# Where the matmul operands of a two-part kernel lie in SBUF, modulo 256 bytes, and two buffers in place of three for one result

## The chip, the cores and the metric

The kernel runs on one core of one Trainium2 chip. The metric is the device time of one execution in microseconds (us). Before the change it is 1865.64 us, the median of three runs (1865.52 to 1867.26). A time below that is faster.

## The reference

For four sequences of 3072 positions with 256 features, three blocks follow one another:

```python
# 1: a real Fourier transform over the sequence, a complex 256x256 mix, soft threshold, inverse
X = np.fft.rfft(x, axis=1)
Yr = Xr @ w_r - Xi @ w_i + b_r
Yi = Xr @ w_i + Xi @ w_r + b_i
Y = sign(Y) * max(abs(Y) - 0.01, 0)          # on Yr and Yi apart
y = np.fft.irfft(Y, n=3072, axis=1)
# 2: 256 -> 2048 -> 256 with h * tanh(softplus(h)) between ("H" below)
h = y @ w_in;  z = (h * np.tanh(np.log1p(np.exp(h)))) @ w_out
# 3: channel mix, 256 -> 1024 -> 256 ("K" below)
xk = mu_k * z + (1 - mu_k) * z_prev;  xr = mu_r * z + (1 - mu_r) * z_prev
v = np.maximum(xk @ w_k, 0) ** 2 @ w_v
out = v / (1 + np.exp(-(xr @ w_r)))
```

`w_in`, `w_out`, `w_k`, `w_v` and the gate's `w_r` arrive as 8-byte floats; the kernel decodes them itself.

## The kernel before, in words

Two functions follow one another. `part1` does block 1, `part2` blocks 2 and 3. All matmuls are issued through `mm` (L211), ScalarE's copies and functions through `act` (L208), VectorE's operations through `tt` (L202) and `stt` (L205); rows are therefore told apart by tile names.

**Part 1** runs 48 steps `u` (4 sequences x 12 tiles of frequencies). In each step TensorE does the forward transform of tile `u + 1` (`emit_F`, PSUM tile `xps`), the mix of tile `u` (`emit_M`, `yps`) and the inverse transform of tile `u - 1` (`emit_I`, `bps`). ScalarE and VectorE work between them, in an order that the code writes out: `post_M` and `post_M2` are the soft threshold (`yb`, first on ScalarE, then on VectorE), `post_F` splits the transformed tile into a high part `xh` (ScalarE) and a low part `xl` (VectorE). `post_I(u - 2)` copies the inverse's result from PSUM to an SBUF tile `bs` (ScalarE) and sends it to DRAM (`b_dr`). `preload` puts the bias into the PSUM tile of a later mix (ScalarE). Between them VectorE works through a background queue: butterflies of the transform's short factor (tiles `a` and `g`) and decoding of weights. Each engine does its instructions strictly in the order in which they were issued. All DMAs are issued by one queue, SP's, in order too. The pool of the tile `bs` has three buffers, and the tile `warm` at the start takes one of them, so that the ScalarE copy of step `u` waits until the DMA of step `u - 3` has landed.

**Part 2** is issued by a planner (`Plan`) that orders steps by due times and estimated costs. Each big product is done as seven products of half-size blocks. Every operand is split into a high and a low fp32r part, and each product is three matmuls: high by high, high by low, low by high. There are two stages:

- H: 96 groups, each with 7 products (21 matmuls into `x`, `z`, `c`, `d`; stationary `wr`, 128 columns, moving `yc`, 512 columns) and 4 units of the second layer (6 matmuls each into `a`; stationary `wo`, moving `h` and `l`, 512 columns).
- K: 48 groups, each with 7 products (21 matmuls; stationary `wk`, moving `yc`, 512 columns), 4 units (12 matmuls each into `v`; stationary `h` and `l`, moving `wv`, 256 columns) and one gate unit (12 matmuls into `zps`; stationary `xr`, moving the gate's weights, 256 columns, which lie in the last `wk` tile of each quadruple).

Every stationary operand has 128 columns, 512 bytes of a partition.

"Place" below means the address within a partition, modulo 256 bytes, counted from the place at which all pools begin: the sizes of the pools are whole multiples of 256 bytes, but for the first small one, so all begin at the same place. Tiles of `mat` (weights) have 512 floats, 2048 bytes: place 0. In stage H everything lies at place 0. In stage K the helper `OFF` moves `yc` by 16 floats, and `outs_of` (its second argument) and the tile `xr` do the same with `h`, `l` and `xr`: place 64. So in stage K before:

- products: stationary `wk` at 0, moving `yc` at 64
- units and gate: stationary `h`, `l`, `xr` at 64, moving `wv` and gate weights at 0

The tiles `fm`, `im` of part 1 (transform matrices) and the weights of part 2 come from the same pool `mat` with 24 buffers, which are used in turn.

Of the kernel before, what the change touches and what calls it, by code (L numbers as in the profile page):

```python
# [11 lines left out]
F32 = mybir.dt.float32  # L12
# [157 lines left out]
def tile_fft_mix_moe_channel_mix(  # L170
# [53 lines left out]
    big = pool(ctx, "big", 2)  # L224
    mat = pool(ctx, "mat", 24)
    g_p = pool(ctx, "g", 1)
# [320 lines left out]
    def wout_piece(i):  # L547
        raw = raw_piece(w_out[256 * i:256 * i + 256, :])

        def parts(q):  # L550
            ts = [mat.tile([128, 2, 256], F32R, tag="m", name="wo") for _ in range(2)]
            wt["out", 2 * i], wt["out", 2 * i + 1] = ts
            return [(ts[k][:, 0, :], ts[k][:, 1, :], q[:, k, :]) for k in range(2)]
        return decode(raw, flat_q, parts)
# [78 lines left out]
    def new_ring(k):  # L633
        for _ in range(4):
            ring.append(mat.tile([128, 4, 128], F32R, tag="m", name="wr"))

# [5 lines left out]
    def part1():  # L642
        with ExitStack() as es:
# [3 lines left out]
            yb_p = pool(es, "yb", 2)  # L647
            bs_p = pool(es, "bs", 3)
            st_p = pools["st"] = pool(es, "st", 2)
# [113 lines left out]
            for i in range(NT + 1):  # L763
                if i < NT:
                    fm[ORD[i]] = mat.tile([128, 2, 256], F32, tag="m", name="fm")
                if 1 <= i:
                    im[ORD[i - 1]] = mat.tile([128, 2, 256], F32, tag="m", name="im")
            new_a(0)
# [64 lines left out]
            for u in range(NU):  # L833
# [62 lines left out]
                if u == NU - 2:  # L896
                    for c in (4, 5, 12, 13, 6, 7, 14, 15):
                        wt["out", c] = mat.tile([128, 2, 256], F32R, tag="m", name="wo")
                    new_ring(0)
                    for k in range(4):  # L900
                        load_ring(0, k)
# [9 lines left out]
    def part2():  # L911
        with ExitStack() as es:
# [8 lines left out]
            NA = 8 * NSB  # L921
            OFF = lambda key: 16 if key >= NSB else 0
            KINDS = [(0, 0), (0, 1), (1, 1), (1, 0)]
# [65 lines left out]

            def outs_of(second, off, f32_of, unit_of, cost):  # L990


                def outs(n, made):
                    b, T = at(n), at(n + 1) - at(n)
                    read = {}
                    for q, kind in enumerate(KINDS):
# [4 lines left out]
                        def tiles(kind=kind, st=st):  # L1001
                            if not st:
                                for i, w in enumerate("hl"):
                                    st[i] = o_p.tile([128, 576], F32R, tag="%s%d%d" % ((w,) + kind), name=w)[:, off:off + 512]
                            return st
# [53 lines left out]

            out_H = outs_of(units, 0, f32_H, unit_H, 1.362)  # L1060

            def moving(key, b0, pace, load, old, *prev):
# [14 lines left out]
                for q, k in enumerate(MOVING):  # L1077
                    def hi(k=k, q=q):
                        if q == 0:
                            mv[key] = big.tile([128, 7232], F32R, tag="big", name="yc")[:, OFF(key):OFF(key) + 7168].rearrange("p (a b f) -> p a b f", a=2, b=7)  # L1080
                        part_hi(mv[key], tl["s"], k)()
                    h = add("ACT", 0.54, b0 + 14 + pace * (q + 1), hi, sums[k] if k < 4 else ld, first or old)
                    first = first or h
                    l = add("DVE", 0.6, b0 + 14 + pace * (q + 1.5), lambda k=k: part_lo(mv[key], tl["s"], k)(), h)
                    res[q] = [h, l]
                    reads += [h, l]
# [172 lines left out]

            kw, vw, have = {}, {}, {}  # L1260
            held = [[units[8 * (NSB - 1) + c % 8, (i, c // 8)] for i in range(2)]
# [5 lines left out]
            for e, ((w, g, k), free) in enumerate(zip(want, held)):  # L1267
                def fetch(w=w, g=g, k=k):
                    if w == "v":
                        vw[g] = mat.tile([128, 2, 256], F32R, tag="m", name="wv")  # L1270
                        nc.sync.dma_start(out=vw[g].bitcast(F32), in_=v_dr[g // 2][:, :, 256 * (g % 2):256 * (g % 2) + 256])
                        return
                    t = mat.tile([128, 4, 128], F32R, tag="m", name="wk")
                    kw.setdefault(g, []).append(t)
                    m = 4 if k < 3 else 2
                    nc.sync.dma_start(out=t[:, 0:m, :].bitcast(F32), in_=k_dr[g][:, 4 * k:4 * k + m, :])
                    if k == 3:
                        s, h = divmod(g, 2)
                        nc.sync.dma_start(out=t[:, 2:4, :].rearrange("p a f -> p (a f)").bitcast(F32),
                                          in_=v_dr[4][:, s, 256 * h:256 * h + 256])  # L1280
# [36 lines left out]

            out_K = outs_of(vunits, 16, f32_K, unit_K, 1.412)

# [5 lines left out]
            def gate_prep(J, b0):  # L1325
                res, first = {}, None
                for i in range(2):
                    s = slice(512 * i, 512 * i + 512)

                    def load(s=s):  # L1330
                        if not xr:
                            xr[0] = g_p.tile([128, 4160], F32R, tag="g", name="xr")[:, 16:4112].rearrange(
                                "p (s h f) -> p s h f", s=2, h=2)
                        nc.sync.dma_start(out=xr[0][:, 1, :, s].bitcast(F32), in_=xr_dr[J].rearrange("h p f -> p h f")[:, :, s])
# [11 lines left out]
            def gate(J, q, need):  # L1346
# [6 lines left out]
                def go():  # L1353
                    ps = tl["p"] = psw.tile([128, 2, 256], F32, tag="z", name="zps")
                    for p in range(2):
                        ts = slice(256 * q + 128 * p, 256 * q + 128 * p + 128)
                        for h in range(2):
                            wh, wl = [kw[2 * s + h][3][:, 2:4, :].rearrange("p a f -> p (a f)") for s in range(2)]
                            xh, xl = [xr[0][:, s, h, ts] for s in range(2)]
# [80 lines left out]
```

## Time and profile before

| | |
|---|---|
| median of the runs | 1865.64 us |
| the profiled execution | 1865.58 us |
| its span, first to last instruction | 1863.8 us |
| TensorE (PE) busy | 1854.4 us, 99% |
| VectorE (DVE) busy | 1413.8 us, 76% |
| ScalarE (ACT) busy | 1197.3 us, 64% |
| mean granted TensorE clock | 1.000 |

Busy time of TensorE counts matmuls from their start to their modelled end, and neighbours overlap; a share of 99% says that a matmul is nearly always under way, not that each goes at the best rate. The rate is read from the starts: the time between the starts of consecutive matmuls. PEld is the loading of stationary operands, which runs beside the matmul before. Idle time of an engine stands with what ended it ("<-").

### The profile page before, as it was taken

To read this page: it belongs to the slowest core of one execution; us is meant where nothing else is said; L and a number is where in the kernel's file an instruction comes from. 1 tells how busy PE (TensorE), PEld (TensorE's weight loads), DVE (VectorE), ACT (ScalarE), POOL (GpSimd) and SP (SyncE) were. 2 spreads that over 40 slices of the span, in tenths; PEclk is the share of its full clock that TensorE was granted. 3 is DMA by queue.
4 is the path that set the end of the run, shared out by engine and by line. 5 is a ranking of instruction groups with operands and counts; after the bars stand their busy time and mean duration, and the time that the engine had idled before them with its cause. 6 is when DMAs were issued, how large, how long until landed. Compare 5 with 4: busy or idle time off the path is not lost.

```text
span 1863.8 us, 26630 instructions
## 1 busy us (share of the span) xinstructions
PE 1854.4 (99%) x9658; PEld 1597.8 (86%) x9658; DVE 1413.8 (76%) x2519; ACT 1197.3 (64%) x2151; POOL 5.9 (0%) x16
## 2 busy tenths in 40 slices
PE   9999999999999999999999999999999999999999
PEld 7888888888888888888888888888999999999998
DVE  7998975898798879697777867666676666666654
ACT  3444376665667657575766657576877777777775
POOL 0000000000000000000000000000000000000000
PEclk9999999999999999999999999999999999999999
DMA  8325185545656554555646455454222222222211
GB/s 299 122 91 195 42 285 184 185 145 172 200 166 196 158 165 145 171 155 157 190 132 203 149 160 174 125 185 145 97 69 68 69 69 68 69 68 69 69 46 34
DMA packets 174274, 255.78 MB, mean 137 GB/s; under 512 B 15552, under 2 KB 99264, under 8 KB 173888
## 3 DMA queue, kind: packets, MB, share of 16 engines
q1 hardware_dynamic: 174144, 254.08, 43.2%
q8 instruction: 77, 1.26, 0.3%
q14 instruction: 53, 0.43, 0.1%
HBM read 177.47 MB, written 76.55 MB: 136 GB/s over the span
## 4 chain that ended last, share of the span: by engine, by line
PE 91%; DVE 7%; DMA 1%; issue 0%; ACT 0%; SPq 0%; DVEq 0%
PE a L211 28%; PE x L211 16%; PE v L211 14%; PE c L211 11%; PE d L211 5%; PE z L211 5%; PE yps L211 4%; PE zps L211 4%; DVE a L202 3%; PE bps L211 3%; PE xps L211 2%; DVE a L205 1%; DVE g L202 1%; DVE xl L202 1%; DVE yb L205 1%
## 5 line engine op out<-in xcount | busy, mean ns | idle before, releaser
L202 DVE TENSOR_TENSOR l<-k,h 128x512 fp32r<-128x512 f32 x576 | 391.3, 688 | 313.0 <-ACT h L208 150.1
L211 PE MATMUL a<-h,wo 128*128 128x512 f32 x1536 | 520.4, 389 | 0.0
L211 PEld LDWEIGHTS a<-h,wo 128*128 128x128 f32 x1536 | 288.3, 188 | 59.8
L211 PE MATMUL a<-l,wo 128*128 128x512 f32 x768 | 298.8, 389 | 0.0
L211 PE MATMUL v<-wv,h 128*128 128x256 f32 x1536 | 274.3, 278 | 0.0
L211 PEld LDWEIGHTS v<-wv,h 128*128 128x128 f32 x1536 | 244.3, 188 | 13.6
L211 PE MATMUL x<-yc,wr 128*128 128x512 f32 x864 | 243.2, 390 | 1.0 <-ACT c L208 1.0
L208 ACT ACTIVATE k<-c 128x512 f32<-128x512 f32 x288 | 172.7, 600 | 105.8 <-PE c L211 93.9
L208 ACT ACTIVATE c<-x 128x512 f32<-128x512 f32 x288 | 169.5, 589 | 92.7 <-PE x L211 78.5
L208 ACT ACTIVATE k<-k 128x512 f32<-128x512 f32 x288 | 178.2, 632 | 64.8 <-DVE k L202 62.3
L211 PE MATMUL v<-wv,l 128*128 128x256 f32 x768 | 213.0, 277 | 0.0
L211 PEld LDWEIGHTS x<-yc,wr 128*128 128x128 f32 x864 | 161.7, 188 | 36.3 <-ACT c L208 2.3
L208 ACT ACTIVATE d<-x 128x512 f32<-128x512 f32 x144 | 84.5, 587 | 147.7 <-PE x L211 146.5
L211 PEld LDWEIGHTS a<-l,wo 128*128 128x128 f32 x768 | 144.2, 188 | 30.2
L211 PE MATMUL c<-yc,wr 128*128 128x512 f32 x576 | 161.8, 389 | 0.0
L211 PEld LDWEIGHTS v<-wv,l 128*128 128x128 f32 x768 | 144.4, 188 | 0.0
L208 ACT ACTIVATE h<-k 128x512 fp32r<-128x512 f32 x192 | 118.7, 629 | 27.9 <-DVE k L205 25.8
L202 DVE TENSOR_TENSOR k<-d,zs 128x512 f32<-128x512 f32 x144 | 98.7, 686 | 44.7 <-PE d L211 44.5
L211 PEld LDWEIGHTS c<-yc,wr 128*128 128x128 f32 x576 | 108.1, 188 | 22.6
L202 DVE TENSOR_TENSOR yc<-src,yc 128x512 fp32r<-128x512 f32 x168 | 111.9, 686 | 15.3 <-ACT yc L208 14.9
L211 PE MATMUL x<-yc,wk 128*128 128x512 f32 x432 | 122.5, 392 | 0.0
L202 DVE TENSOR_TENSOR g<-g 128x128 f32<-128x128 f32 (+3 forms) x264 | 110.5, 441 | 0.8
(104 smaller groups left out, 2785.9 us busy)
## 6 DMA issues: line engine op xcount, KB each, us to landing
wr<-h_dr SPq DMA_DIRECT2D x288, 256.0 KB, 2.7
b_dr<-bs SPq DMA_DIRECT2D x48, 256.0 KB, 2.2
src<-y_dr SPq DMA_DIRECT2D x24, 512.0 KB, 4.2
wr<-h_dr SPq DMA_DIRECT2D x96, 128.0 KB, 2.1
xk_dr<-tm SPq DMA_DIRECT2D x48, 256.0 KB, 2.9
xr_dr<-tm SPq DMA_DIRECT2D x48, 256.0 KB, 3.2
src<-xk_dr SPq DMA_DIRECT2D x24, 512.0 KB, 4.2
xr<-xr_dr SPq DMA_DIRECT2D x24, 512.0 KB, 3.8
```

The costliest lines, as they stand in the source:

```text
L202: V.tensor_tensor(out=o, in0=a, in1=b, op=op)
L205: V.scalar_tensor_tensor(out=o, in0=a, scalar=s, in1=b, op0=op0, op1=op1)
L208: S.activation(out=o, in_=i, func=f, **kw)
L211: T.matmul(out=o, lhsT=l, rhs=r, start=start, stop=stop, **kw)
```

## The change

Three things are changed.

- The pool `mat` hands out its 24 buffers in the same turn as before, but through a helper `slot`, which makes 12 of them 576 floats wide (2304 bytes, nine times 256) and leaves 12 at 512. The buffers that will hold `wv` and the last `wk` tile of a quadruple are the wide ones. `wv` is put 48 floats into its buffer (place 192), and the gate's weights from float 304 on (place 192).
- The offsets of 16 floats are gone: `yc`, `h`, `l` and `xr` of stage K lie at place 0. So all stationary operands of part 2 lie at place 0, moving operands with 512 columns too, and moving operands with 256 columns at place 192, 64 bytes below the next multiple of 256.
- `mat` grows by 3072 bytes of each partition; the pool of `bs` gets two buffers in place of three (2048 bytes less). The tiles `h` and `l` shrink from 576 to 512 floats, `xr` from 4160 to 4096.

No matmul, activation, vector operation or DMA is added or taken away.

```diff
--- before.py
+++ after.py
@@ -222,7 +222,18 @@
...
     big = pool(ctx, "big", 2)
-    mat = pool(ctx, "mat", 24)
+    mat = pool(ctx, "mat", 12)
+    slots = [0]
+
+    def slot(dtype, name):
+        i = slots[0] % 24
+        slots[0] += 1
+        wide = i in (3, 4, 5, 6, 7, 11, 15, 16, 17, 18, 19, 23)
+        t = mat.tile([128, 576 if wide else 512], dtype, tag="w" if wide else "m", name=name)
+        return t
+
+    def slot3(dtype, name, k):
+        return slot(dtype, name)[:, 0:512].rearrange("p (k f) -> p k f", k=k)
     g_p = pool(ctx, "g", 1)
...
@@ -548,7 +559,7 @@
...
         def parts(q):
-            ts = [mat.tile([128, 2, 256], F32R, tag="m", name="wo") for _ in range(2)]
+            ts = [slot3(F32R, "wo", 2) for _ in range(2)]
             wt["out", 2 * i], wt["out", 2 * i + 1] = ts
...
@@ -632,7 +643,7 @@
...
         for _ in range(4):
-            ring.append(mat.tile([128, 4, 128], F32R, tag="m", name="wr"))
+            ring.append(slot3(F32R, "wr", 4))
 
...
@@ -645,7 +656,7 @@
...
             yb_p = pool(es, "yb", 2)
-            bs_p = pool(es, "bs", 3)
+            bs_p = pool(es, "bs", 2)
             st_p = pools["st"] = pool(es, "st", 2)
...
@@ -762,9 +773,9 @@
...
                 if i < NT:
-                    fm[ORD[i]] = mat.tile([128, 2, 256], F32, tag="m", name="fm")
+                    fm[ORD[i]] = slot3(F32, "fm", 2)
                 if 1 <= i:
-                    im[ORD[i - 1]] = mat.tile([128, 2, 256], F32, tag="m", name="im")
+                    im[ORD[i - 1]] = slot3(F32, "im", 2)
             new_a(0)
...
@@ -895,7 +906,7 @@
...
                     for c in (4, 5, 12, 13, 6, 7, 14, 15):
-                        wt["out", c] = mat.tile([128, 2, 256], F32R, tag="m", name="wo")
+                        wt["out", c] = slot3(F32R, "wo", 2)
                     new_ring(0)
...
@@ -919,7 +930,6 @@
...
             NA = 8 * NSB
-            OFF = lambda key: 16 if key >= NSB else 0
             KINDS = [(0, 0), (0, 1), (1, 1), (1, 0)]
...
@@ -987,7 +997,7 @@
...
 
-            def outs_of(second, off, f32_of, unit_of, cost):
+            def outs_of(second, f32_of, unit_of, cost):
 
...
@@ -1001,7 +1011,7 @@
...
                                 for i, w in enumerate("hl"):
-                                    st[i] = o_p.tile([128, 576], F32R, tag="%s%d%d" % ((w,) + kind), name=w)[:, off:off + 512]
+                                    st[i] = o_p.tile([128, 512], F32R, tag="%s%d%d" % ((w,) + kind), name=w)
                             return st
...
@@ -1057,7 +1067,7 @@
...
 
-            out_H = outs_of(units, 0, f32_H, unit_H, 1.362)
+            out_H = outs_of(units, f32_H, unit_H, 1.362)
 
...
@@ -1077,7 +1087,7 @@
...
                         if q == 0:
-                            mv[key] = big.tile([128, 7232], F32R, tag="big", name="yc")[:, OFF(key):OFF(key) + 7168].rearrange("p (a b f) -> p a b f", a=2, b=7)
+                            mv[key] = big.tile([128, 2, 7, 512], F32R, tag="big", name="yc")
                         part_hi(mv[key], tl["s"], k)()
...
@@ -1257,7 +1267,7 @@
...
 
-            kw, vw, have = {}, {}, {}
+            kw, vw, gw, have = {}, {}, {}, {}
             held = [[units[8 * (NSB - 1) + c % 8, (i, c // 8)] for i in range(2)]
...
@@ -1267,16 +1277,18 @@
...
                     if w == "v":
-                        vw[g] = mat.tile([128, 2, 256], F32R, tag="m", name="wv")
+                        vw[g] = slot(F32R, "wv")[:, 48:560].rearrange("p (k f) -> p k f", k=2)
                         nc.sync.dma_start(out=vw[g].bitcast(F32), in_=v_dr[g // 2][:, :, 256 * (g % 2):256 * (g % 2) + 256])
                         return
-                    t = mat.tile([128, 4, 128], F32R, tag="m", name="wk")
+                    full = slot(F32R, "wk")
+                    t = full[:, 0:512].rearrange("p (k f) -> p k f", k=4)
                     kw.setdefault(g, []).append(t)
...
                         s, h = divmod(g, 2)
-                        nc.sync.dma_start(out=t[:, 2:4, :].rearrange("p a f -> p (a f)").bitcast(F32),
+                        gw[g] = full[:, 304:560]
+                        nc.sync.dma_start(out=gw[g].bitcast(F32),
                                           in_=v_dr[4][:, s, 256 * h:256 * h + 256])
...
@@ -1315,7 +1327,7 @@
...
 
-            out_K = outs_of(vunits, 16, f32_K, unit_K, 1.412)
+            out_K = outs_of(vunits, f32_K, unit_K, 1.412)
 
...
@@ -1329,8 +1341,7 @@
...
                         if not xr:
-                            xr[0] = g_p.tile([128, 4160], F32R, tag="g", name="xr")[:, 16:4112].rearrange(
-                                "p (s h f) -> p s h f", s=2, h=2)
+                            xr[0] = g_p.tile([128, 2, 2, 1024], F32R, tag="g", name="xr")
                         nc.sync.dma_start(out=xr[0][:, 1, :, s].bitcast(F32), in_=xr_dr[J].rearrange("h p f -> p h f")[:, :, s])
...
@@ -1355,7 +1366,7 @@
...
                         for h in range(2):
-                            wh, wl = [kw[2 * s + h][3][:, 2:4, :].rearrange("p a f -> p (a f)") for s in range(2)]
+                            wh, wl = [gw[2 * s + h] for s in range(2)]
                             xh, xl = [xr[0][:, s, h, ts] for s in range(2)]
...
```

## Rows read from the trace of the kernel before

**Rows 1.** Span and mean granted clock of the core.

```profile
core 0: 1863.8 us, clock 1.000
```

**Rows 2.** Three stretches (part 1, H, K): length, busy time and instructions by engine, granted clock, DMA share, GB/s.

```profile
30.00:320.00 290.00, 288.63 (x1346) 246.97 (x1346) 246.84 (x429) 143.44 (x270) 0.10 (x1) 1.00 0.47 155
340.00:1280.00 940.00, 940.00 (x4147) 778.07 (x4147) 741.90 (x1415) 600.15 (x1068) 5.62 (x11) 1.00 0.54 166
1320.00:1860.00 540.00, 539.73 (x3749) 500.55 (x3747) 362.93 (x574) 400.54 (x714) 0.00 (x0) 1.00 0.20 65
```

**Rows 3.** PE in order of time, stage K: start, length, line, tiles, count.

```profile
1502.05 0.39 PE L211 MATMUL v<-wv,h 128*128 128x256 f32 x2
...
1502.73 0.85 PE L211 MATMUL x<-yc,wk 128*128 128x512 f32 x3
...
1504.10 0.40 PE L211 MATMUL v<-wv,h 128*128 128x256 f32 x2
...
1505.49 0.85 PE L211 MATMUL x<-yc,wk 128*128 128x512 f32 x3
```

**Rows 4.** PE groups of the stretch 1320 to 1860: tiles, shape, count, busy, mean ns.

```profile
L211 PE MATMUL v<-wv,h 128*128 128x256 f32 x1480 | 264.5, 278 | 0.0
L211 PE MATMUL v<-wv,l 128*128 128x256 f32 x740 | 205.3, 277 | 0.0
L211 PE MATMUL x<-yc,wk 128*128 128x512 f32 x407 | 115.4, 392 | 0.0
L211 PE MATMUL c<-yc,wk 128*128 128x512 f32 x273 | 77.3, 391 | 0.0
L211 PE MATMUL zps<-wk,xr 128*128 128x256 f32 x576 | 73.8, 277 | 0.0
L211 PE MATMUL d<-yc,wk 128*128 128x512 f32 x138 | 39.0, 391 | 0.0
L211 PE MATMUL z<-yc,wk 128*128 128x512 f32 x135 | 38.2, 391 | 0.0
```

**Rows 5.** PE in order of time where H and K are interleaved, first and last row.

```profile
1291.11 0.87 PE L211 MATMUL x<-yc,wk 128*128 128x512 f32 x3
...
1303.62 0.40 PE L211 MATMUL v<-wv,h 128*128 128x256 f32 x2
```

**Rows 6.** ACT in order of time, part 1: start, length, tiles [idle before <- releaser].

```profile
175.78 0.59 ACT L208 ACTIVATE bs<-bps 128x512 f32<-128x512 f32 x1
...
185.41 0.60 ACT L208 ACTIVATE bs<-bps 128x512 f32<-128x512 f32 x1 [3.34 <-DMA b_dr<-bs]
...
186.42 0.59 ACT L208 ACTIVATE yb<-yps 128x512 f32<-128x512 f32 x1
```

**Rows 7.** The one store of bs issued at 175.2: time to landing.

```profile
L759 SPq DMA_DIRECT2D b_dr<-bs x1: 379/379/379, 175.2 to 175.2; - x1
...
DMA to landing us min/median/max: 10.2/10.2/10.2
```

**Rows 8.** DVE in order of time, part 1.

```profile
181.59 0.68 DVE L205 SCALAR_TENSOR_TENSOR yb<-yps,yb 128x512 f32<-128x512 f32 x1
...
232.86 0.68 DVE L205 SCALAR_TENSOR_TENSOR yb<-yps,yb 128x512 f32<-128x512 f32 x1
```

**Rows 9.** DVE in the stretch 178 to 234: length, busy time.

```profile
178.00:234.00 56.00, 55.45 (x96) 1.00 0.26 91
```

**Rows 10.** PE in order of time, inverse transforms (bps) of two steps in part 1.

```profile
184.00 1.89 PE L211 MATMUL bps<-im,yb 128*128 128x256 f32 x8
...
233.59 1.99 PE L211 MATMUL bps<-im,yb 128*128 128x256 f32 x8
```

**Rows 11.** Stretches at both ends: PE busy (x count) first, then the granted clock.

```profile
1.40:6.40 5.00, 4.95 (x12) 3.96 (x13) 0.07 (x1) 0.62 (x1) 0.00 (x0) 1.00 0.92 281
1859.00:1863.00 4.00, 0.73 (x7) 0.53 (x5) 1.37 (x2) 0.00 (x0) 0.00 (x0) 1.00 0.52 176
1863.00:1863.80 0.80, 0.00 (x0) 0.00 (x0) 0.00 (x0) 0.00 (x0) 0.00 (x0) 0.66 0.00 0
```

## The prediction

> **What bounds the kernel now.** I read the span and the busy times by stage first, then the starts of TensorE's matmuls in stage K and where H and K mix, then ScalarE, VectorE and SP around the copies of the inverse's result, because the change touches the places of operands in part 2 and one buffer in part 1. The profiled execution took 1865.58 us (span 1863.8 [rows 1]), the median of the runs is 1865.64; the sum below is made against 1865.58, and 0.06 us between the two changes nothing.
>
> TensorE is busy in 288.63 of 290 us of part 1, in all 940 of H, in 539.73 of 540 of K [rows 2]. VectorE and ScalarE have idle time in H and K (741.9 and 600.2 of 940; 362.9 and 400.5 of 540). So what counts is how far apart matmuls start. In H 4147 matmuls of 512 columns, all operands at one place, take 940.00 us: 226.67 ns each [rows 2]. This is the clean price of 512 columns. In K, six matmuls of 256 columns from 1502.05 to 1502.73 take 0.68 us, 113.3 ns each, the last six of their unit of twelve; the unit of twelve at 1504.10 takes 1.39 us to 1505.49, where twelve at 113.3 would take 1.36; the six of 512 columns before it, 1502.73 to 1504.10, take 1.37 against 1.36 clean [rows 3]. So K loses some 0.04 us in each such round: the 512s go slower than in H, and a unit of 256s that follows them starts slow and then settles.
>
> How much that is: the stretch 1320 to 1860 holds 407 + 273 + 138 + 135 = 953 matmuls of 512 columns and 1480 + 740 + 576 = 2796 of 256 [rows 4]. At the clean prices they take 953 x 0.22667 + 2796 x 0.11333 = 216.0 + 316.9 = 532.9 us; the stretch has 540. The loss is 7.1 us. The whole stage has 48 x 21 = 1008 and 48 x 60 = 2880, so 7.1 x 2880 / 2796 = 7.3 us.
>
> **The change, part by part.** *Places.* In K before, the products have their moving operand at 64 and the stationary at 0; units and gate have the moving at 0 and the stationary at 64. The load of the next stationary operand runs beside the current matmul, so at a change from products to a unit a matmul moving from 64 has a load from 64 beside it, and back from 0 with 0. After, each load comes from 0: beside 512 moving columns from 0, as everywhere in H, and beside 256 from 192. A unit before has 0 against 64, that is 64 below, and after 192 against 0, again 64 below modulo 256. So a product gets the relation that runs at 226.67 in H, and a unit keeps the one in which it settles at 113.3. The two clean prices are 2 to 1 as the columns are, so an alternation of both has a step in common, and I expect no settling between them.
>
> The bounds: at best both clean prices hold everywhere, -7.3 us. At worst a mixture of moving places unsettles both. The nearest row is the passage where H and K interleave: there all stationary operands lie at 0 and 512-column moving operands at 64 (`yc` of K) and at 0 alternate. 54 matmuls (30 of products, 24 into `a`) take 1291.11 to 1303.62, 12.51 us, 231.7 ns each [rows 5], and none settles at 226.67. Products now take 1.37 us for six, 228.3 ns each [rows 3]; if all 1008 went at 231.7 and the units stayed as they are, that would cost 3.4 ns x 1008 = +3.4 us. I take -7.3: both relations of after, unlike that of 64, are ones the rows show settled.
>
> *Buffers.* With three, the copy of `bs` of step u waits for the store of step u - 3 to land, with two for that of u - 2. In most steps this is nothing: 48 steps share some 290 us [rows 2], so two of them leave a store 12 us. Not so around 180. The store issued at 175.2 lands 10.2 us later [rows 7], at 185.4; it is queued behind the loads of x for the last sequence (`new_a`). Before, it holds up the copy three steps after it, at 185.41, after 3.34 us of idle time; the copy before that one went through at 175.78 [rows 6]. With two buffers it is that copy, two steps after the store, that waits until 185.41: 9.6 us. Behind it on ScalarE stand a bias preload, the first half of a soft threshold (`yb`), the split `xh`. The gaps between the rows at 185.41 and 186.42 [rows 6] place this `yb` at 186.42 to 187.01 in the new order too, for it follows the copy and one preload.
>
> Who waits: VectorE's half of that `yb`, at 181.59 before [rows 8], cannot start before 187.05 (the 187.01 of ScalarE and a few hundredths for the hand-over): 5.46 us late, and all behind it in VectorE's order with it. TensorE's inverse transform at 184.00 [rows 10] needs it finished, 187.05 + 0.68 = 187.73: a gap of 3.7 us. VectorE then has no idle time to catch up: from 178 to 234 it is busy in 55.45 of 56 us [rows 9]. The `yb` that starts at 232.86 ends at 233.54 [rows 8], and the inverse transform behind it starts at 233.59 [rows 10], 0.05 us later. So TensorE's delay grows from 3.7 to 5.46 - 0.05 = 5.4 us by then. After it TensorE is the bound to the end [rows 2], so nothing gives it back. The bounds: 5.46 less all the idle time in the stretch, 4.9, and 5.5 if the landing comes a little later; 0 if the store lands earlier.
>
> *The rest.* The number of instructions and DMAs is as before. The 24 buffers of `mat` are used in the same turn, so no wait on them is new. 2304 is nine times 256, so `fm`, `im` and H keep their places. These cost nothing, with no cover needed.
>
> Sum: 1865.6 - 7.3 + 5.4 = 1863.7 us.
>
> **The rivals.**
>
> *Places do nothing; slower.* If the 229-like pace of K comes from something else than the places (say from 256 and 512 columns alternating), K stays and the buffer costs 5.4: 1871.0. For it: only K has both widths. Against it: the interleaved passage has 512 columns alone and goes at 231.7 [rows 5], and the products of H, with the same steps, at 226.67 [rows 2]. It decides wherever the gain in K is below 5.4 - 3.7 = 1.7 us. The Trainium skill (SBUF — State Buffer, "Who interferes with whom") says that the PE has two independent read ports, for moving operand and weight load, and "PE and ACT never wait on anyone"; by that rule places cannot matter and the time would be 1871.0, but the passage of [rows 5] speaks against it.
>
> *Only part of the gain.* The 512s go clean, but each unit still starts slow: with 0.01 us of 0.04 gained per round [rows 3], about 2 of 7.3 us: 1869.
>
> *The buffer costs little; faster.* If the store at 175.2 lands sooner in most executions, or the copy is not held as I read it, -7.3 stands nearly alone: 1858.3 to 1860. For it: this is one landing in one execution. Against it: what stands ahead of the store in SP's queue is the same in each.
>
> *The clock falls.* A gap of 3.7 us may cost TensorE its higher clock level. The granted clock stays 1.00 in the 4 us from 1859, of which TensorE is busy 0.73, and shows a mean of 0.66 in the last 0.80 us [rows 11]. A fall from 1.00 to 0.50 at 1863.26 gives that mean (0.26 us at 1.00, 0.54 at 0.50), 3.5 us after work ended at 1859.73: the gap is about as long. At the start, 12 matmuls of 128x256 take 5 us [rows 11], 417 ns each, where 8 take 1.89 at 184 [rows 10], at most 236. If the low level (1.2 GHz in place of 2.4) lasted through as many, 12 x 236 = 2.8 us of work would take 5: 2.2 us lost, 1865.9. VectorE's lateness would cover part of it, so this lies between 1863.7 and 1865.9. The Trainium skill (TensorE: Matmul & The Clock Gate, "Why this matters for your kernels") warns of idle gaps between bursts of matmuls for this reason; no row shows a gap like it within the work.
>
> **How the numbers follow.** Full gain with the full wait 0.53 (1863.7, own range 1861.5 to 1866), full gain and a fallen clock 0.09 (1865.9), places do nothing or harm 0.13 (1871 and above), part of the gain 0.10 (1869), buffer costs little 0.15 (1858.3 to 1860). A measurement tells 0.2%, 3.7 us, from no change: faster is below 1861.9, slower above 1869.4. Faster: 0.15 and 0.04 of the likeliest's lower edge, 0.19; slower: 0.13 and 0.03 of the partial gain, 0.16; the rest, 0.65, is within. The range 1858.8 to 1871 leaves out the lower half of the one side and the worst of the other.
>
> **What would show it.** Right: 953 and 2796 matmuls in K as here at 226.7 and 113.3, also the first five of a unit, the stage some 7 us shorter; in part 1 a ScalarE wait of about 9.6 us for `b_dr<-bs` near 176, a TensorE gap of 3 to 4 us near 184, and stage H starting some 5.4 us later. Wrong: units of twelve still at 1.39 us; products at 229 or more; no wait at 176; a granted clock below 1.00 after the gap.

## The result, and the profile after

The changed kernel takes 1877.62 us (median; 1876.74 to 1878.64), the kernel before 1865.4 beside it: ratio 1.0065, 95% interval 1.0055 to 1.0075. It is slower by 12.2 us, where 1.9 us less was forecast, and outside the range. The profiled execution took 1877.45 us, 11.87 more than that of before.

Both kernels issue 9658 matmuls, so the start of each can be set against the start of the same one before. How late it is, in us, at matmuls that stand at these times in the kernel before:

| before's matmul at | 183 | 234 | 316 | 328 | 1290 | the last |
|---|---|---|---|---|---|---|
| changed kernel | -0.19 | 5.54 | 5.56 | 6.31 | 6.31 | 11.73 |

The loss comes in three steps: TensorE is 5.56 us late by 316, nearly all of it gained between 183 and 234; 0.75 us come between 316 and 328, and 5.42 in stage K. H adds nothing. Each step is shown with its rows.

**The buffer.** ScalarE in order of time, changed kernel:

```profile
185.47 0.60 ACT L208 ACTIVATE bs<-bps 128x512 f32<-128x512 f32 x1 [9.77 <-DMA b_dr<-bs]
185.96 0.60 ACT L208 ACTIVATE yps<-bias 128x512 f32<-128x512 f32 x1
186.48 0.59 ACT L208 ACTIVATE yb<-yps 128x512 f32<-128x512 f32 x1
```

This is the copy that went through at 175.78 in [rows 6]. It now waits until the landing that held up the next copy before, and `yb` stands behind it. VectorE and TensorE after it, one fence for each engine, in order of time:

```profile
187.10 0.69 DVE L205 SCALAR_TENSOR_TENSOR yb<-yps,yb 128x512 f32<-128x512 f32 x1 [5.36 <-ACT yb L208]
```

```profile
187.85 3.46 PE L211 MATMUL bps<-im,yb 128*128 128x256 f32 x8 [3.87 <-DVE yb L205]
191.14 0.59 PE L211 MATMUL xps<-fm,a 128*128 128x256 f32 x2
...
239.13 1.99 PE L211 MATMUL bps<-im,yb 128*128 128x256 f32 x8
```

VectorE's half of `yb` starts 5.51 us later than in [rows 8], the inverse transform 3.85 us later than in [rows 10], and the one at 239.13 is 5.54 late (233.59 in [rows 10]).

**The clock.** The eight matmuls at 187.85 take 3.29 us to the next start; those at 184.00 took at most 1.89 [rows 10]. Windows of the changed kernel (length, busy time of PE, PEld, DVE, ACT and POOL with their instructions, then granted clock, DMA share, GB/s):

```profile
183.80:187.40 3.60, 0.18 (x1) 0.00 (x0) 0.30 (x1) 1.93 (x4) 0.00 (x0) 1.00 0.26 91
187.50:190.80 3.30, 2.95 (x7) 2.42 (x8) 3.30 (x4) 1.55 (x4) 0.00 (x0) 0.50 0.33 108
190.90:196.00 5.10, 5.10 (x24) 4.30 (x24) 5.10 (x7) 1.85 (x4) 0.00 (x0) 1.00 0.15 54
```

From about the end of the gap the granted clock was at its lower level (0.50, 1.2 of 2.4 GHz), and it rose again some 3.4 us later. VectorE was the later of the two in any case: its half of `yb` is 5.51 us late, and TensorE at 234 is 5.54 late, so nothing of the lower clock is left there.

**Where part 2 begins.** ScalarE and then TensorE near 324, changed kernel:

```profile
323.93 0.60 ACT L208 ACTIVATE zs<-z 128x512 f32<-128x512 f32 x1 [1.25 <-DMA b_dr<-bs]
```

```profile
323.53 0.86 PE L211 MATMUL c<-yc,wr 128*128 128x512 f32 x3
325.07 0.73 PE L211 MATMUL x<-yc,wr 128*128 128x512 f32 x2 [0.68 <-ACT d L208]
```

The same two matmul groups in the kernel before:

```profile
317.97 0.86 PE L211 MATMUL c<-yc,wr 128*128 128x512 f32 x3
318.80 0.97 PE L211 MATMUL x<-yc,wr 128*128 128x512 f32 x3
```

0.83 us from `c` to `x` became 1.54. `mat` is larger and the pool of `bs` smaller, so the tile `zs` of part 2 now lies where a buffer of `bs` lay, and its first copy waits for the last store from there.

**Stage K.** TensorE in order of time, changed kernel:

```profile
1510.85 0.84 PE L211 MATMUL x<-yc,wk 128*128 128x512 f32 x3
1511.53 0.84 PE L211 MATMUL z<-yc,wk 128*128 128x512 f32 x3
1512.21 0.40 PE L211 MATMUL v<-wv,h 128*128 128x256 f32 x2
...
1513.62 0.39 PE L211 MATMUL x<-yc,wk 128*128 128x512 f32 x1
```

Six of 512 columns take 1.36 us (1.37 in [rows 3]): clean. Twelve of 256 take 1.41 (1.39 in [rows 3]), 117.5 ns each, and no part of a unit settles. The stretch 1331 to 1871 and the groups of matmuls in it:

```profile
1331.00:1871.00 540.00, 540.00 (x3719) 503.31 (x3718) 357.91 (x567) 396.69 (x707) 0.00 (x0) 1.00 0.20 65
```

```profile
L211 PE MATMUL v<-wv,h 128*128 128x256 f32 x1469 | 267.7, 281 | 0.0
L211 PE MATMUL v<-wv,l 128*128 128x256 f32 x735 | 206.8, 281 | 0.0
L211 PE MATMUL x<-yc,wk 128*128 128x512 f32 x402 | 113.0, 389 | 0.0
L211 PE MATMUL c<-yc,wk 128*128 128x512 f32 x270 | 75.8, 389 | 0.0
L211 PE MATMUL zps<-wk,xr 128*128 128x256 f32 x576 | 75.7, 281 | 0.0
L211 PE MATMUL d<-yc,wk 128*128 128x512 f32 x135 | 37.9, 390 | 0.0
L211 PE MATMUL z<-yc,wk 128*128 128x512 f32 x132 | 37.1, 389 | 0.0
```

3719 matmuls in 540 us where [rows 2] show 3749. 939 of them have 512 columns, 2780 have 256: (540 - 939 x 0.22667) / 2780 = 117.7 ns. The mean length of a 256 rose from 278 to 281 ns ([rows 4]), that of a 512 fell from 391 to 389. From its first start to its last, K went from 568.35 to 573.76 us: over all, the 512s gave 2.5 us and the 256s took 7.9 (331.1 to 339.1).

### The profile page after: what moved, and what is told of

It reads as the page before. It is cut to its first block, busy times and chain, and to the rows that moved or that the text cites. A ratio compares the mean times of both kernels' runs of the same rounds, so it can differ in the third digit from the quotient of the medians.

```text
span 1875.5 us, 26647 instructions
## 1 busy us (share of the span) xinstructions
PE 1861.8 (99%) x9658; PEld 1607.3 (86%) x9658; DVE 1414.4 (75%) x2519; ACT 1197.1 (64%) x2151; POOL 5.9 (0%) x16
## 4 chain that ended last, share of the span: by engine, by line
PE 90%; DVE 7%; DMA 1%; ACT 1%; SPq 0%; issue 0%; DVEq 0%
PE a L211 28%; PE x L211 16%; PE v L211 14%; PE c L211 10%; PE d L211 5%; PE z L211 5%; PE zps L211 4%; PE yps L211 3%; DVE a L202 3%; PE bps L211 3%; PE xps L211 2%; DVE a L205 1%; DVE g L202 1%; DVE xl L202 1%; DVE yb L205 1%; DMA b_dr<-bs 1%
## 5 line engine op out<-in xcount | busy, mean ns | idle before, releaser
L211 PE MATMUL v<-wv,h 128*128 128x256 f32 x1536 | 279.7, 281 | 0.0
```

Source lines behind the costliest of these rows:

```text
L211: T.matmul(out=o, lhsT=l, rhs=r, start=start, stop=stop, **kw)
```

## The experiments

Two readings of K stood against each other at first: the pace of a matmul is set by how far its own moving operand lies from its own stationary one (*own pair*), or by what lies about it as well, the next load and the other width (*sequence*). Beside them: the two costs outside K, each by itself. "Products" are the 512s of K, "units" its 256s. The table has every kernel that computes the whole, with the lateness as in the table above (three of its columns). Each ratio is to runs of the kernel before beside it (medians 1865.23 to 1865.89). K is counted from its first matmul to the start of its last; 27 of H's matmuls of 512 columns lie within it and are in that mean.

| kernel | median us | ratio to before, 95% | at 234 | at 328 | last | K us | mean of 512, 256 in K, ns |
|---|---|---|---|---|---|---|---|
| before | 1865.4 | | 0 | 0 | 0 | 568.35 | 229.2, 115.0 |
| changed | 1877.62 | 1.0065 [1.0055, 1.0075] | 5.54 | 6.31 | 11.73 | 573.76 | 226.8, 117.8 |
| e1 | 1871.0 | 1.0030 [1.0019, 1.0041] | 5.32 | 5.34 | 5.41 | 568.35 | 229.2, 115.0 |
| e2 | 1872.34 | 1.0037 [1.0023, 1.0051] | -0.11 | -0.07 | 6.47 | 574.97 | 231.0, 116.7 |
| e3 | 1877.24 | 1.0063 [1.0048, 1.0078] | 5.14 | 5.88 | 11.17 | 573.71 | 226.7, 117.8 |
| e4 | 1881.68 | 1.0088 [1.0073, 1.0103] | 4.57 | 5.30 | 15.57 | 578.61 | 232.0, 117.6 |
| e5 | 1867.97 | 1.0014 [1.0005, 1.0023] | 6.44 | 7.15 | 3.06 | 564.25 | 229.1, 113.6 |
| e6 | 1861.88 | 0.9981 [0.9972, 0.9991] | 0.53 | 1.28 | -2.83 | 564.25 | 229.1, 113.6 |
| e7 | 1871.14 | 1.0030 [1.0018, 1.0042] | -0.56 | 0.15 | 5.46 | 573.71 | 226.7, 117.8 |
| e8 | 1876.22 | 1.0057 [1.0044, 1.0070] | -0.64 | 0.07 | 10.03 | 578.36 | 231.2, 117.8 |
| e9 | 1875.43 | 1.0053 [1.0039, 1.0066] | 0.11 | 0.12 | 10.28 | 578.37 | 231.1, 117.8 |
| e10 | 1861.43 | 0.9980 [0.9971, 0.9989] | 0.07 | 0.11 | -3.97 | 564.25 | 229.1, 113.6 |

**e1: the buffer alone**, in the kernel before.

```diff
-            bs_p = pool(es, "bs", 3)
+            bs_p = pool(es, "bs", 2)
```

> The kernel before with two buffers for the inverse's result and no other change. Theory 'buffer' (the copy two steps after the store issued near 175 waits for its landing, VectorE carries the lateness, TensorE does not get it back): +5 to +6 us over before, a ScalarE wait of 9 to 10 us for b_dr<-bs near 176, stage H some 5.5 us later, and stage K as long as before. Rival 'the buffer costs more than its own wait' (the 12 us of the change are mostly the buffer's): +9 us or more. Rival 'buffer is hidden': within 1 us of before.

5.5 us slower, and K as before. ScalarE, e1:

```profile
185.25 0.60 ACT L208 ACTIVATE bs<-bps 128x512 f32<-128x512 f32 x1 [9.44 <-DMA b_dr<-bs]
```

The buffer's price is settled. There is no step between 316 and 328 here: that one belongs to the new layout.

**e2: `yc` at 0**, the only change to the kernel before; `h`, `l`, `xr` stay at 64.

```diff
-            OFF = lambda key: 16 if key >= NSB else 0
+            OFF = lambda key: 0
```

> The kernel before with yc of stage K at place 0 in place of 64, no other change (wk 0, h, l and xr 64, wv and gate weights 0). Products then have relation 0 as in H. Theory 'place of the pair' (where the moving and the stationary operand of a unit lie decides its rate, whatever ran before): products 226.7 ns, units settle at 113.3 as before, total -2.5 to -7 us. Theory 'what runs before' (products at relation 0 leave a step from which units do not settle, products at 64 do not): products 226.7, units 117.5 to 118 throughout as in the changed kernel, stage K some 5 us longer, total +5 us.

Now the products' own pair is at distance 0, the clean one, and the units' own pair is untouched. Both get slower: 231.0 and 116.7 ns. By *own pair* the one should have gained and the other stayed. What decides shows within this one execution. TensorE in order of time, e2:

```profile
1514.63 0.86 PE L211 MATMUL c<-yc,wk 128*128 128x512 f32 x3
1515.33 0.39 PE L211 MATMUL v<-wv,h 128*128 128x256 f32 x2
...
1516.69 0.86 PE L211 MATMUL x<-yc,wk 128*128 128x512 f32 x3
...
1518.08 0.40 PE L211 MATMUL v<-wv,h 128*128 128x256 f32 x2
...
1519.49 0.86 PE L211 MATMUL x<-yc,wk 128*128 128x512 f32 x3
```

The unit behind three 512s takes 1.36 us, 113.3 ns a matmul; the one behind six takes 1.41, 117.8. It is so throughout K: of the units into `v` that follow products, all 54 behind three 512s run at 113.3 and all 106 behind six or more at 117.8. The pair and its places are the same, and what ran before differs. So each of the two forecasts was right for some units only, and both missed the products (226.7 expected).

**e3: everything 64 bytes further** in the changed kernel, distances kept.

```diff
-    mus = cst.tile([128, 64], F32, name="mus")
+    mus = cst.tile([128, 80], F32, name="mus")
```

> The changed kernel with every tile moved up by 64 bytes (the first small pool is 64 bytes longer), so all relations between operands stay and all places move: units then have the moving operand and the stationary at the same two absolute places as in the kernel before. Theory 'absolute place' (the pair of absolute places decides): units settle at 113.3 ns as before, total 7 to 8 us below the changed kernel. Theory 'what runs before' or any that knows only differences of places: units stay at 117.5 to 118, total as the changed kernel within 1 us.

K takes 573.71 us, as changed. A shift of all places by 64 bytes changes nothing in K: it is the places relative to each other that count.

**e4: the changed kernel with `yc` at 64.**

```diff
+            OFF = lambda key: 16 if key >= NSB else 0
...
-                            mv[key] = big.tile([128, 2, 7, 512], F32R, tag="big", name="yc")
+                            mv[key] = big.tile([128, 7232], F32R, tag="big", name="yc")[:, OFF(key):OFF(key) + 7168].rearrange("p (a b f) -> p a b f", a=2, b=7)
```

> The changed kernel with yc of stage K at place 64, so products have the relation that they had before (moving 64 above the stationary) and units that of the changed kernel. Theory 'what runs before': units settle at 113.3 after their first five, products at 229, total 5 to 6 us below the changed kernel. Theory 'place of the pair': units stay at 117.5 to 118, products at 229, total 2 to 3 us above the changed kernel.

Worse than either: 578.61 us in K. A thought that units settle because the products beside them move from 64 falls with it.

**m1: matmuls alone.** Two tiles in SBUF; no other engine works beside the matmuls, and the only transfers are the output's stores in the first 65 us. m1, and m2 and m3 below, were executed once each. First steady runs at sixteen distances (`wide`: 512 columns, `thin`: 256; the last letter counts steps of 16 bytes), then 64 sets of places. A set is one matmul and six rounds of six 512s and twelve 256s, as in K; the letters of `k...` are the places of `yc`, of `h` and of `wv` (a 0, b 64, c 128, d 192), with `wk` at 0.

```python
for r in range(6):
    products(o, 16 * y, 0, 2)
    unit(o, 16 * v, 16 * s, 4)
```

> A kernel of matmuls alone that leaves out the whole computation of the reference (its output is no result). First 21 matmuls of 512 columns, then 30 of 256, at each of 16 distances of the moving operand from the stationary one (0 to 240 bytes in steps of 16). Then, for each of the 64 sets of places of yc, of h and l and of wv (0, 64, 128, 192; wk at 0), six rounds of two products (six matmuls of 512 columns) and one unit (twelve of 256), as in stage K. A clean round takes 6 x 0.2267 + 12 x 0.1133 = 2.72 us, six 16.3. Theory 'two steps' (units have two steady paces at the same places, 113.3 and 117.7 ns, and how a run enters decides): the set of the kernel before (yc 64, h 64, wv 0) has units near 115.3, the set of the changed kernel (0, 0, 192) 117.7 throughout, that of e2 (0, 64, 0) near 116.3, and a run of 256 alone at distance 192 has one of the two paces. Rival 'something outside TensorE' (writes of ScalarE and VectorE into SBUF, or addresses beyond 256 bytes, make the difference): with TensorE alone these sets no longer differ.

Steady runs: 512 columns go at 226.7 ns at distance 0 alone, at 228.8 at 64, and at 230 to 236.7 elsewhere; 256 columns at 113.3 at distance 192, settling to the same at 112, and at 117 to 120 elsewhere. TensorE in order of time, m1; each row starts one run, and what counts is the time to the next start:

```profile
120.88 3.80 PE L186 MATMUL thine<-mov,sta 128*128 128x256 f32 x30
124.74 3.82 PE L186 MATMUL thinf<-mov,sta 128*128 128x256 f32 x30
...
151.83 3.68 PE L186 MATMUL thinm<-mov,sta 128*128 128x256 f32 x30
155.57 3.84 PE L186 MATMUL thinn<-mov,sta 128*128 128x256 f32 x30
...
219.57 17.15 PE L186 MATMUL kaad<-mov,sta 128*128 128x512 f32 x109
236.78 17.30 PE L186 MATMUL kaba<-mov,sta 128*128 128x512 f32 x109
...
462.84 16.91 PE L186 MATMUL kbab<-mov,sta 128*128 128x512 f32 x109
479.81 17.44 PE L186 MATMUL kbac<-mov,sta 128*128 128x512 f32 x109
497.31 17.30 PE L186 MATMUL kbad<-mov,sta 128*128 128x512 f32 x109
514.66 17.07 PE L186 MATMUL kbba<-mov,sta 128*128 128x512 f32 x109
531.79 0.50 PE L186 MATMUL kbbb<-mov,sta 128*128 128x512 f32 x1
```

Alone, `thinm` (distance 192, that of the changed units) takes 3.74 us, `thine` (64) 3.86. In rounds it turns round: `kaad` (the changed set) takes 17.21 us with units at 117.8, `kbab` (all moving at 64, all stationary at 0) 16.97 with units at 113.3, the least of the 64. `kbba` (before) takes 17.13, `kaba` (e2) and `kbad` (e4) 17.35 each. Before, changed, then e2 and e4 is the order of the kernels too. With the paces of these rounds (before 229.0 and 115.5 ns, changed 226.7 and 117.8) K would lose 2880 x 2.3 - 1008 x 2.3 ns = 4.3 us, of the 5.4 measured: most of K's loss needs nothing but TensorE and the places. And a pair's pace alone says nothing of its pace in a round. One forecast was missed: e2's units go at 117.8 here and not near 116.3. These rounds have six 512s throughout, where the kernel has three at times.

The Trainium skill (SBUF — State Buffer, "Who interferes with whom") has it that "PE and ACT never wait on anyone". No run here disagrees as to other engines. As to TensorE's own two operands the measurement decides: nothing but their distance differs between 226.7 and 236.7 ns in these steady runs.

**e5: the best of the 64 in the kernel**: e4, with `wv` and the gate's weights at 64 as well.

```diff
-                        vw[g] = slot(F32R, "wv")[:, 48:560].rearrange("p (k f) -> p k f", k=2)
+                        vw[g] = slot(F32R, "wv")[:, 16:528].rearrange("p (k f) -> p k f", k=2)
...
-                        gw[g] = full[:, 304:560]
+                        gw[g] = full[:, 272:528]
```

> The changed kernel with all moving operands of stage K, yc of 512 columns and wv and gate weights of 256, at place 64 and all stationary ones at 0: the set that was shortest with TensorE alone (products 228.9 ns, units 113.3). Theory 'two steps, set by the whole round' (the places of both operands of both kinds decide together which pace the units have, and TensorE alone shows it): products 228.9 to 229.2, units 113.3 from the first matmul on, stage K 10 to 11 us shorter than in the changed kernel (2880 x 4.4 ns less 1008 x 2.2 ns), total about 1867. Rival 'distance 64 is bad for 256 columns' (a run of 256 columns alone at 64 takes 117.8): units 117.5 to 118, products 229 or more, total 1880.

K takes 564.25 us, 4.1 less than before and 9.5 less than changed; the units run at 113.6 in the mean, the products as before. They do not do so from the first matmul on. TensorE in order of time, e5:

```profile
1340.19 0.40 PE L211 MATMUL v<-wv,h 128*128 128x256 f32 x2
...
1341.61 0.87 PE L211 MATMUL c<-yc,wk 128*128 128x512 f32 x3
...
1344.46 0.39 PE L211 MATMUL v<-wv,h 128*128 128x256 f32 x2
...
1345.82 1.52 PE L211 MATMUL zps<-wk,xr 128*128 128x256 f32 x12
```

Up to 1342 all units go at 117.9 ns (1.42 us here) and the products at about 231. Then comes a gate unit whose first weight load waits 0.22 us for ScalarE. From the next unit on, units go at 113.3 (1.36 us) and products at 228.8, to the end of K. e6 and e10 change pace at the same gate unit. In the changed kernel that load waits too (0.23 us), but only the two units behind it are faster, 115 and 113; after the next products they are back at 117.8. In e8 (below) it waits 0.22 us and changes nothing.

The buffer's cost remains, and the kernel ends 2.5 us behind before. In its profile the clock stayed low for longer (window as above):

```profile
186.70:193.40 6.70, 5.75 (x14) 4.60 (x15) 6.50 (x7) 2.15 (x5) 0.00 (x0) 0.50 0.25 81
```

Here the lateness grows by 6.9 us from 183 (-0.42) to 234 (6.44), against 5.7 in the changed kernel's profile: VectorE, whose `yb` is 5.35 us late there, no longer covers all of it. The profiles of e3 and e4 have the two buffers too, with gaps on TensorE of 2.67 us (e3) and 3.30 us (e4). Behind the first the clock was low, behind the second it was not (first row e3, second e4):

```profile
187.60:190.90 3.30, 3.30 (x8) 2.56 (x9) 3.30 (x4) 1.03 (x3) 0.00 (x0) 0.50 0.27 84
186.90:190.90 4.00, 4.00 (x19) 3.51 (x20) 4.00 (x4) 1.38 (x4) 0.00 (x0) 1.00 0.22 70
```

**e6: e5 with three buffers** for `bs`; one buffer of `raw` (set in three places) pays for the space.

```diff
-            bs_p = pool(es, "bs", 2)
+            bs_p = pool(es, "bs", 3)
...
-        raw = pools["st"].tile([128, 512, 2], I32, tag="raw", name="raw", bufs=4)
+        raw = pools["st"].tile([128, 512, 2], I32, tag="raw", name="raw", bufs=3)
```

> The same with three buffers for the inverse's result; the room comes from one buffer less (three for four) of the raw weights in part 1. Theory 'buffer': no wait of ScalarE for b_dr<-bs over 4 us and stage H 5.5 us earlier than in e5, so about 1861, some 4.5 us below the kernel before. Rival 'the raw weights wait for their buffer in place of it': no gain over e5.

3.5 us faster than before: K's gain stands alone, less the step at `zs`.

**e7: the changed kernel with the diff of e6**: the places without the buffer.

> The changed kernel's places with three buffers for the inverse's result (three in place of four buffers of raw weights). Theory 'buffer' and 'two steps': the two parts add, so 5.5 us below the changed kernel, about 1871.5, and still 6 us above before, all of it in units at 117.5 to 118 ns. Rival 'the places cost nothing': as before.

5.7 us slower than before, all of it in K and at `zs`. With e1's 5.5 that makes 11.2 of the 12.2. The last 1.0 isn't traced: the profiles of e6, e7 and e8, with the same part 1, already differ by as much at 234 (0.53, -0.56, -0.64). e5's longer spell of low clock would fit the two longest executions of the changed kernel (1878.09 and 1878.64 us, with the lowest mean clocks, 0.997 and 0.998), but the profiled one doesn't show such a spell.

**m2: all stationary operands at 0**, moving ones of products and units at every multiple of 16 bytes, 256 sets like those of m1.

```python
for y in range(16):
    for v in range(16):
...
            products(o, 4 * y, 0, 2)
            unit(o, 4 * v, 0, 4)
```

> Matmuls alone, the computation of the reference left out: four rounds of two products and a unit for each of 256 sets of places of yc and wv in steps of 16 bytes, all stationary operands at 0 as the change has them. Theory 'two steps': the changed kernel's set (0, 192) takes 2.77 us a round with units at 117.7, the set (64, 64) 2.73 with units at 113.3, and few sets have units at 113.3. Rival 'an offset of 64 bytes is enough': all sets with wv 64 bytes off in either direction have units at 113.3.

Read in the third round, eight of the 256 have units under 113.7 ns. One round alone went wholly clean: products from 112, units from 64, 2720 ns, which is 6 x 226.67 + 12 x 113.33. The changed set took 2773 again (226.7, 117.8). But the set of e5 showed units of 117.8 here, and 113.3 in m1 and in e5: the same places, two paces.

**e8: `yc` at 112**, e6 otherwise, to have the clean round of m2.

```diff
-            OFF = lambda key: 16 if key >= NSB else 0
+            OFF = lambda key: 28 if key >= NSB else 0
```

> As e6, but yc of stage K at place 112 in place of 64 (wv and gate weights at 64, all stationary operands at 0, three buffers): the one set of the 256 with TensorE alone in which both kinds ran clean (2720 ns a round, products 226.7, units 113.3). Theory 'two steps, set by the whole round': the same in the kernel, products 226.7 and units 113.3 to 113.5, stage K 2 us shorter than in e6, total about 1859.5 to 1860. Rival 'a set so rare does not hold where rounds differ in length' (rounds of one to three products, gate units between): products 229 or more, or units 117, total 1862 or above.

A miss: 578.36 us in K, units at 117.8, products at 231.2. m2's clean round didn't carry over.

**e9: e8 with two pools of part 2 in the other order**, so that `zs` (pool `f`) lies elsewhere.

```diff
-            f_p = pool(es, "f", 1)
             x_p = pool(es, "x", 1)
+            f_p = pool(es, "f", 1)
```

> As e8, with the pools of part 2 called f and x allocated in the other order, so that the tile zs no longer lies where the buffers of bs lay. Theory 'overlap' (in the changed layout the first copy into zs waits 1.3 us for the last store of bs, which delays TensorE by 0.8 us at the start of stage H): that wait is gone and the total 0.5 to 0.9 us below e8. Rival 'hidden': the wait goes and the total stays within 0.3 us.

The step between 316 and 328 is gone (0.12 and 0.12, where e8 goes from -0.62 to 0.07). The medians differ by 0.8 us, about the size of the step.

**m3: the same sets, entered in different ways.** Six sets of places, each run 32 times, each time behind twelve matmuls of another width or distance (`pre...`); then one matmul and four rounds.

```python
for k in range(12):
    mm(o[:, 0:cols], sta[:, 128 * (k % 4):128 * (k % 4) + 128], mov[:, 4 * d:4 * d + cols], k == 0)
...
for r in range(4):
    products(o, y, 0, 2)
    unit(o, v, s, 4)
```

> Matmuls alone, the computation of the reference left out. Six sets of places (yc, h, wv; wk at 0): of the kernel before (64, 64, 0), the changed one (0, 0, 192), e5 (64, 0, 64), e8 (112, 0, 64), e2 (0, 64, 0), e4 (64, 0, 192), each entered after 32 different runs of twelve matmuls of one width and distance, then four rounds. Theory 'places decide': a set has the same round from the third on after every run before it, 2.76, 2.77, 2.73, 2.72, 2.80, 2.80 us. Theory 'history' (a set has several paces that hold themselves, and what ran before picks one): at least e8's set, which took 2.72 alone and 117.8 ns a unit matmul in the kernel, comes out with two or more rounds depending on the run before; for the changed set the question is open: if it too has an entry after which units go at 113.3, its places are not at fault by themselves.

Read in the third round: before's set 22 times 2760 ns (units 115.5) and 10 times 2807 (117.8). The changed set: units at 117.8 in all 32. The set of e5: 15 times 2733 (113.3), 17 times 2787 or 2800 (117.8). That of e8: once 2720, 31 times 2800. Those of e2 and e4: 2800 in all 32. TensorE in order of time, m3, the set of e5 behind two of its entries:

```profile
884.36 11.34 PE L186 MATMUL setcwa<-mov,sta 128*128 128x512 f32 x73
895.54 0.62 PE L186 MATMUL precwb<-mov,sta 128*128 128x512 f32 x2
...
898.32 11.53 PE L186 MATMUL setcwb<-mov,sta 128*128 128x512 f32 x73
909.69 0.63 PE L186 MATMUL precwc<-mov,sta 128*128 128x512 f32 x2
```

The same 73 matmuls at the same places take 11.18 us behind `precwa` and 11.37 behind `precwb`. So a set has one pace or several that hold themselves, and what ran before chooses.

**e10: e6 with the pools in e9's order** (the diff of e9).

> As e6 (moving operands of stage K at 64, stationary at 0, three buffers) with the two pools of part 2 in the other order, as in e9. Theory 'overlap': 0.6 to 0.9 us below e6, about 1861.1, some 4.5 us below before, with units at 113.3 to 113.5. Rival 'history': the start of stage H shifts the entry and units come out at another pace, 1863 or above.

1861.43 us, 3.8 less than before, the fastest kernel of the study. The step at `zs` is gone in its profile (0.09 at 316, 0.11 at 328), but the median is only 0.45 us below that of e6, where 0.6 to 0.9 was expected. TensorE in order of time, e10:

```profile
1516.30 0.85 PE L211 MATMUL x<-yc,wk 128*128 128x512 f32 x3
1516.99 0.85 PE L211 MATMUL c<-yc,wk 128*128 128x512 f32 x3
1517.68 0.39 PE L211 MATMUL v<-wv,h 128*128 128x256 f32 x2
...
1519.04 0.85 PE L211 MATMUL x<-yc,wk 128*128 128x512 f32 x3
```

The twelve 256s of this unit take 1.36 us, clean from the first on; the six 512s take 1.38. The mirror image of the changed kernel, and the better half, as K has 2880 of the 256s and 1008 of the 512s.

## Why the prediction was wrong

*What bounds the kernel*: right. H did not move, and each loss on TensorE's path came through to the end.

*Places*: this step failed, at two sentences. "I expect no settling between them", and "I take -7.3: both relations of after, unlike that of 64, are ones the rows show settled". A relation was read there as the property of a matmul's own pair, so that the pace of a unit in the kernel before would follow it to other places. The products did go clean, -2.5 us. The units lost 7.9 in place of gaining: 117.8 ns from start to end, and not the 113.3 to which they came within each unit before. e2 (a pair left as it was gets slower, and in one execution goes at 113.3 behind three 512s and at 117.8 behind six), e4, and m1 (the pair that is fastest alone is slow in rounds) refute *own pair*. What is shown in its place: the pace belongs to the whole round of widths and places (m1), it holds itself, and some sets of places have two such paces, chosen by what ran before (m3). The changed set showed only the slow one for units in all 32 entries; before's set and e5's have both kinds.

The forecast's worst case erred in the same way. It let the products go slow and left the units as they were, +3.4; what happened was the reverse, and +5.4.

*Buffers*: right. +5.4 was forecast; e1 measured +5.5. The wait was 9.77 us (9.6 forecast), the gap on TensorE 3.87 (3.7), the lateness at 234 5.54.

*The rest* "cost nothing": wrong by 0.7 us. The turn of `mat` was looked at, but not what else moves when a pool grows: `zs` came to lie on a buffer of `bs` that a store was still reading. e9 and e10 take it away by the order of two pools.

*The rivals.* "Places do nothing" is refuted, since the products changed their pace. "Only part of the gain" has one half right, clean products, and missed that the units would lose. "The clock falls" happened: the granted clock was 0.50 for some 3.4 us behind the gap, and cost nothing more there, since VectorE was later still; in e5's profile it left TensorE 1.1 us behind VectorE. The Trainium skill's warning (TensorE: Matmul & The Clock Gate, "Why this matters for your kernels") agrees with that row: a gap between bursts did cost the level. In e4 a gap of 3.30 us did not. The forecast took its price of the lower level from the first 5 us, 417 ns for 128x256, but that row of [rows 11] gives a granted clock of 1.00; the changed kernel's eight matmuls at 0.50 do show it: 3.29 us, 411 ns each. "The buffer costs little" is refuted by e1.

Sum as measured in the profiles: 5.56 + 0.75 + 5.42 = 11.73 of 11.87 us.

What stays open: why some combinations of widths and places have a slow pace that holds itself. The experiments show that TensorE, the relative places and what ran before are enough for it; they show nothing of how the two operands' reads meet. The places in m1 to m3 lie within one stretch of 256 bytes, so that 256 is the period is taken over here, not measured. In e5, e6 and e10 K changes to the fast pace right behind one late weight load, and in e8 it stays slow behind the same one. That this load is what picks the pace was not tested by itself; in m3 the fast pace came in 15 of 32 entries for e5's set and in 1 of 32 for e8's, which fits.

## What to carry to other kernels

The pace of a matmul that is read in one sequence is no price to move into another: when places or widths beside it change, run the new round by itself, behind several different runs, and count only on a pace that holds behind most of them. Moving operands at one common place and stationary ones at another gave the best K here, though neither pair is the fastest alone. A buffer less, or a pool larger, is costed at the one late store, and by asking which tiles come to lie where others lay.

## What the runs showed of the hardware

- The distance of moving and stationary operand, modulo 256 bytes, sets the pace of a steady run of matmuls: 226.7 to 236.7 ns for 512 columns, 113.3 to 120.0 for 256 (m1). The best distance is 0 for the one width and 192 for the other (112 comes to the same pace after some matmuls).
- The same matmuls at the same places ran at two lasting paces, according to what ran before them: 2733 and 2787 or 2800 ns a round (m3). Within one execution, units at the same places went at 113.3 ns behind three matmuls of 512 columns and at 117.8 behind six (e2).
- Behind a gap of 3.9 us within the work, the granted clock was 0.50 for some 3.4 us in one profile and for 6.8 in another (changed, e5); behind one of 2.67 us it was 0.50 too (e3), and behind one of 3.30 us it stayed at 1.00 (e4).
